# Token MLP of the first row's pairs within that row: more steps per iteration, the third pair too, and another copy on ScalarE

## The chip, the cores and the metric

The kernel runs on one core of one Trainium2 chip. The metric is the device time of one execution in microseconds. Three runs of the kernel before took 1360.49, 1360.82 and 1363.06 us; the median, 1360.82 us, is what the changed kernel is compared with. The profiled execution took 1359.68 us, of which 1357.6 us lie between the first and the last instruction. Times in the trace count from the first instruction.

## The reference

Attention with a threshold comes first, then a mixer MLP over tokens and over channels, all in float32. There are 8 batch rows, 8 heads, 576 tokens, head size 64, so a row is a 576 x 512 matrix for the MLPs.

```python
scores = matmul(q, k.T) / sqrt(64)
thresh = max(scores, axis=-1) - tau
scores = where(scores >= thresh, scores, -1e9)
attn = exp(scores - max(scores, axis=-1))
attn = attn / (sum(attn, axis=-1) + 1e-9)
x = matmul(attn, v)                          # heads side by side: 8 x 576 x 512
h = maximum(x.transpose(0, 2, 1) @ w_tok1, 0) @ w_tok2      # 576 -> 256 -> 576, over tokens
u = x + h.transpose(0, 2, 1)
out = u + maximum(u @ w_ch1, 0) @ w_ch2                     # 512 -> 1536 -> 512, over channels
```

The token MLP treats every channel by itself. So it can be made for a pair of heads (128 channels) as soon as the attention of that pair is done for all tokens; the channel MLP needs all four pairs of a row.

## The kernel before

*Units.* Heads are taken two at a time (a pair, 128 channels). The main loop (from L568) runs over 144 units of 128 queries, 18 per batch row: units 0 to 8 are pairs 0 and 1 of row 0, units 9 to 17 its pairs 2 and 3, and so on. Unit 4 of each nine is shared: 64 queries of one pair and 64 of the next. The order of all instructions on every engine is written by hand, by the order of the calls in the loop; each engine takes its own queue in that order.

*One iteration u.* `scores(u)` makes the score matmuls on PE (L303), the row maxima on DVE (L308) and a bias on GpSimd (L309). `weigh(u)` makes Prelu (L318) and Exp (L325) on ScalarE. `norm(u - 1)` takes reciprocals on DVE (L332, L333) and multiplies on GpSimd (L336). Then unit u - 2 is turned, so that keys lie on the partitions. In row 0 `turn` does that on PE in three parts of three transposes each (L354), each part copied from PSUM by DVE or by ScalarE (L356). From row 1 on `turn_blocks` does it by a transposition of blocks on DVE (L366) and, after every third unit, 16 DMAs issued by SyncE (L375).

*Values.* After every third unit `values` multiplies with v on PE (L409, L414). In row 0 this is at u = 5, 8, 11, 14, 17 and 20, called visits; the result is copied to the tile `xT` by DVE (L421). After u = 11 pairs 0 and 1 of row 0 are complete, after u = 17 pair 2, after u = 20 pair 3. In a visit, `weigh(u)` is called ahead of the turns.

*Token MLP.* `token_mlp` returns a list of steps, each with the cost in microseconds that the planner takes for it: transposes on PE (L445) that ScalarE copies to `x_sb` (L446); two steps `tok1` of PE matmuls (L452) with a relu on ScalarE (L453); and steps `tok2` (L459) that DVE adds to `xT` (L463), two for each pair.

*Where the steps run.* `push(b)` (L533), after a row is complete, queues steps in `todo`; `fill` runs them in later iterations, a share of `quota` at a time, so that the queue is spread over the next 18 iterations (less 20 us of it after row 0, `KEEP_FIRST`, and 45 us after later rows). Row 0 has a queue of its own, `early`: after u = 11 the steps of pairs 0 and 1 go there (L601), and in each iteration without a visit one of them is taken (L587): at u = 12, 13, 15, 16, 18 and 19. What is left goes to `todo` at u = 20, with the steps of pairs 2 and 3 and then the channel MLP of the first two chunks of 256 tokens (`ch1`: L483, L484; `ch2`: L499).

*PSUM.* Two buffers with the tag "tr" serve the turns, the values, the transposes of the token MLP and, until u = 18, also `tok1` and `tok2`. Row 0 has a third score buffer (`ps_3rd`); at u = 18 it is given up, and two buffers "mm" take the matmuls of both MLPs. From then on the score matmuls of u wait until Prelu of u - 1 has read its buffers.

*Weights.* All weights arrive as 64-bit numbers. In rows 0 and 1 they are brought to float32 by `weight`: a load (L177), two steps on ScalarE (L192, L194), three on DVE (L202, L204, L208) and one on GpSimd (L216) for each of 31 pieces. Row 0 takes 2.25 DVE steps per iteration; from u = 18 on it is six, two ahead of the turns, two after, two at the end. `prep` transposes q and k of the next pair on DVE (L285).

Of the kernel before, what the change touches and what calls it, by code (L numbers as in the profile page):

```python
# [21 lines left out]
def kernel(  # L22
# [25 lines left out]
    nc = tc.nc  # L48
# [10 lines left out]
    NP = H // 2  # L59
# [26 lines left out]
    UB = 9 * NP // 2  # L86
# [137 lines left out]
    def weight(n):  # L224

        nonlocal steps_done
        for k in range(steps_done, min(steps_done + n, 3 * len(pieces) + 1)):
            i, part = divmod(k, 3)
            if part == 0:
                on_gpsimd(i - 1)  # L230
                if i:
                    load_piece(i - 1 + NRAW)
            else:
                on_scalar(i + 1, part - 1)
            on_vector(i, part)
            steps_done = k + 1

    def weight_to(x):

        weight(max(int(x) - steps_done, 0))  # L240
# [36 lines left out]
    def in_blocks(b):  # L277
        return b > 0
# [50 lines left out]
    def norm(u):  # L329
        e, rs = st[u]  # L330
        rr = small.tile([P, 2], F32, tag="rr", name=f"rr_{u}")
        nc.vector.tensor_scalar(out=rr, in0=rs, scalar1=1e-9, scalar2=None, op0=ALU.add)  # L332
        nc.vector.reciprocal(out=rr, in_=rr)  # L333
        for h in range(2):
            eh = e[:, S * h : S * h + S]
            nc.gpsimd.tensor_scalar(out=eh, in0=eh, scalar1=rr[:, h : h + 1], scalar2=1.0, op0=ALU.mult, op1=ALU.mult)  # L336
        st[u] = e

    GU = 3

    def turn(u, third):

        b, p0, t = units[u]
        key, place = (b, p0, t // GU), t % GU
        e = st[u]

        if third == 0 and place == 0:
            eTs[key] = work.tile([P, NK, GU * P], F32, tag="T", name=f"eT_{u}")
        if third == 2:
            st.pop(u)  # L350
        ps = ps_tr.tile([P, MAIN], F32, tag="tr", name=f"tr{third}_{u}")[:, 0 : 3 * P].rearrange("p (c x) -> p c x", c=3)
        for c in range(3):
            k0 = (3 * third + c) * P
            nc.tensor.transpose(out=ps[:, c, :], in_=e[:, k0 : k0 + P], identity=ident)  # L354
        on = nc.scalar.copy if third == 1 else nc.vector.tensor_copy
        on(out=eTs[key][:, 3 * third : 3 * third + 3, P * place : P * place + P], in_=ps)  # L356

    def turn_blocks(u):
# [18 lines left out]
    def split_middle(n):  # L377

        lv, vl = vals[n], vlast[n % VL]
        for h in range(2):  # L380
            r = slice(D * h, D * h + D)
            nc.gpsimd.tensor_copy(out=vl[r, r], in_=lv[r, NI, :])
        vals[n] = lv, vl
# [144 lines left out]
            credit = 0.0  # L528


    early = deque()

    def push(b):  # L533
        nonlocal quota
        uT = xTs[b]
        steps, waits = token_mlp(b) if b else token_mlp(b, range(NP // 2, NP))
        old = list(todo)
        todo.clear()
        todo.extend(early)
        early.clear()  # L540

        for i, step in enumerate(steps):
            n = 2 if i in waits else 1
            todo.extend(old[:n] + [step])
            del old[:n]
        todo.extend(old)
        for i in range(2) if b % 2 == 0 else range(2, (2 * S + GR - 1) // GR):
            todo.extend(channel_mlp(b - b % 2, uT, i))
        quota = (sum(c for c, _ in todo) - (KEEP if b else KEEP_FIRST)) / (UB - 1)
# [6 lines left out]
    def values_due(u):  # L556
        while due and due[0][0] <= u:
            _, b, p0, g = due.popleft()
            values(b, p0, g)
            if b == 0 and p0 == 0 and g == 2:  # L560
                return True
            if p0 == NP - 2 and g == 2:
                if not in_blocks(b):
                    return True
                push(b)
        return False

    for u in range(len(units) + LAG + 4):  # L568
        on = u < len(units)
        if u == UB:  # L570
            late.close()
            ps_mm = ctx.enter_context(tc.tile_pool(name="ps_mm", bufs=2, space=bass.MemoryType.PSUM))
        if on:
            b_now, p0, t = units[u]
            n = b_now * NP + p0
        w = u - LAG
        back = 0 <= w < len(units)
        if on:
            scores(u)

        last = False
        visit = False
        if due and not in_blocks(due[0][1]):
            visit = due[0][0] <= u
            last = values_due(u)
        elif early:
            early.popleft()[1]()  # L587
        if 0 < u <= len(units):
            norm(u - 1)
        if b_now:  # L590
            weight(2)
        else:


            weight_to(2.25 * (u - (1 if visit else 1.5)))
            if visit and on:
                weigh(u)
        while copies:
            copies.popleft()()
        if last and u < UB:  # L600
            early.extend(token_mlp(0, range(NP // 2))[0])  # L601
        elif last:
            push(0)
        if back:
            wb, wp, wt = units[w]
            if not in_blocks(wb):
                for i in range(3):
                    turn(w, i)
            if wt % GU == GU - 1:
                g = wt // GU  # L610
                if g < 2:
                    split_middle(wb * NP + wp + g)
                due.append((u + (2 if in_blocks(wb) else 1), wb, wp, g))
        if b_now:
            fill(0.4)
        if back and in_blocks(wb):
            turn_blocks(w)
        if b_now:
            weight(2)
        if on and (b_now or not visit):  # L620
            weigh(u)
        elif b_now:
            fill(0.6)
        if b_now:
            weight(2)
        elif u == 0:
            on_scalar(0, 0)
            on_scalar(0, 1)
        else:
            weight_to(2.25 * (u - 1))  # L630
        if on:


            when = {3: (2, 0, 2), 4: (2, 2, 4), 5: (2, 4, 6), 6: (2, 6, 8), 8: (3, 0, 3), 0: (1, 3, 6), 1: (1, 6, 8)}
            if u == 0:
                load_qk(1, (nc.sync, nc.sync), range(0, 3))
            if t in when:
                m, lo, hi = when[t]
                if n + m < len(pairs):
                    load_qk(n + m, (nc.scalar if b_now else nc.sync,) * 2, range(lo, hi))  # L640
            if t in (3, 7) and n + 2 + t // 4 < len(pairs):
                load_v(n + 2 + t // 4)
            if t == 2:
                prep(n + 1)
            if t == 7 and n + 2 < len(pairs):
                prep(n + 2)
        if due and in_blocks(due[0][1]):
            values_due(u)
# [31 lines left out]
```

## Time and profile before

| part of the profile | value |
|---|---|
| span, median time | 1357.6 us, 1360.82 us |
| PE, DVE, ACT, POOL busy | 97%, 42%, 43%, 26% |
| score matmuls of u = 0, 12, 18, 20 start at | 7.14, 64.42, 98.50, 112.08 us |
| of u = 21, 24, 27, 36 | 125.36, 148.59, 173.37, 238.66 us |
| PE idle from 57.65 to 112.08 us | 54.43 - 45.37 = 9.1 us |
| PE idle from 112.08 to 183.68 us | 71.60 - 66.02 = 5.6 us |
| L452, 10 matmuls of 256 columns, at u = 16 | 2.4 us |
| L459, 12 matmuls (three steps), at u = 20 | 3.2 us |

A line of the timeline gives start and duration in microseconds, engine, line of the code, operation, output and inputs, shapes and a count; in brackets stands how long the engine was idle before it and what ended that. PEld are the weight loads of PE, which overlap its matmuls. In the trace one float32 matmul of the code is two matmuls, so a `tok1` step is 10 and a `tok2` step 4. A window's line gives, for each engine, busy time and count of instructions, then the granted clock of PE, the share of the DMA engines and GB/s. In the chain of waits each piece is the work or wait that the next one was released by.

### The profile page before, as it was taken

The numbers are of one execution on the slowest core, as the hardware profiler recorded it, in microseconds if no ns is written. First come the engines' busy times: TensorE is split into PE (matmuls) and PEld (weight loads), VectorE is DVE, ScalarE is ACT, GpSimd is POOL, SyncE is SP. The second block draws the span as 40 slices with busy tenths as digits, with TensorE's granted clock in tenths as the row PEclk, the third lists the DMA queues.
The fourth block names the chain that finished last, engine by engine and source line by source line (L and its number), as shares of the span: only waits on it lengthen the run. The fifth ranks groups of instructions, "written<-read, shape, count | busy, mean of one in ns | idle before, by whom it ended". The sixth has DMA issues, their size and how long they took to land.

```text
span 1357.6 us, 17717 instructions
## 1 busy us (share of the span) xinstructions
PE 1314.2 (97%) x6246; PEld 816.6 (60%) x6246; DVE 576.6 (42%) x1008; ACT 585.5 (43%) x1300; POOL 354.1 (26%) x683
## 2 busy tenths in 40 slices
PE   6888999999999999999999999999999999999998
PEld 4555656547474656655665566565756576576675
DVE  6889864454444434443333454434333443201000
ACT  6776655445454444543434445343434444120010
POOL 4565643222322222221212222221212222100000
PEclk8998999999999999999999999999999999999999
DMA  5435774545453533533254445435333442400000
GB/s 122 117 95 134 198 166 98 128 95 118 104 127 79 131 90 89 131 80 86 66 119 93 103 98 117 96 75 117 89 92 73 116 98 70 111 0 16 8 16 16
DMA packets 278872, 128.21 MB, mean 94 GB/s; under 512 B 200896, under 2 KB 271552, under 8 KB 278784
## 3 DMA queue, kind: packets, MB, share of 16 engines
q1 hardware_dynamic: 150176, 111.06, 32.1%
q10 hardware_dynamic: 128608, 16.01, 7.4%
q8 instruction: 50, 0.82, 0.3%
q14 instruction: 38, 0.31, 0.1%
HBM read 43.25 MB, written 9.44 MB: 39 GB/s over the span
## 4 chain that ended last, share of the span: by engine, by line
PE 86%; DVE 6%; DMA 2%; ACT 2%; SPq 2%; issue 1%; POOL 1%; ACTq 0%; DVEq 0%; POOLq 0%
PE c L499 27%; PE c L483 26%; PE sc L303 10%; PE pv L414 8%; PE t L452 5%; PE t L459 4%; PE pv L409 3%; SPq L375 2%; DVE mx L308 2%; PE tx L445 1%; PE c L495 1%; DMA lk<-in_k_dram 1%; ACT e L318 1%; ACT e L325 1%; PE tr L354 1%
## 5 line engine op out<-in xcount | busy, mean ns | idle before, releaser
L308 DVE TENSOR_REDUCE mx<-sc 128x1 f32<-128x576 f32 x288 | 204.3, 750 | 482.8 <-PE sc L303 482.8
L483 PE MATMUL c<-xT,wc 128*128 128x256 f32 (+1 forms) x1920 | 400.1, 362 | 0.5 <-ACT g L484 0.4
L499 PE MATMUL c<-wc,g 128*128 128x512 f32 x864 | 390.6, 597 | 0.0
L483 PEld LDWEIGHTS c<-xT,wc 128*128 128x128 f32 x1920 | 334.1, 190 | 71.0 <-issue 30.8
L309 POOL TENSOR_SCALAR bias<-mx,toff 128x1 f32<-128x1 f32 x288 | 82.0, 285 | 779.4 <-DVE mx L308 724.7
L318 ACT ACTIVATE e<-sc,bias 128x576 f32<-128x576 f32 x288 | 199.5, 740 | 157.5 <-POOL bias L309 154.8
L499 PEld LDWEIGHTS c<-wc,g 128*128 128x128 f32 x864 | 157.4, 190 | 175.4 <-issue 173.7
L484 ACT ACTIVATE g<-c 128x256 f32<-128x256 f32 (+1 forms) x240 | 87.1, 363 | 321.6 <-PE c L483 295.2
L325 ACT ACTIVATE e<-e,ntau 128x576 f32<-128x576 f32 x288 | 221.0, 771 | 0.0
L336 POOL TENSOR_SCALAR e<-e,rr 128x576 f32<-128x576 f32 x288 | 215.1, 760 | 14.7 <-DVE rr L333 3.0
L303 PE MATMUL sc<-kT,qT 64*128 64x288 f32 (+1 forms) x1280 | 190.5, 432 | 12.4 <-DVE kT L285 7.1
L366 DVE STREAM_TRANSPOSE T<-e 128x1152 f32<-128x1152 f32 x126 | 172.0, 1365 | 6.1 <-DMA eT<-T 3.7
L303 PEld LDWEIGHTS sc<-kT,qT 64*128 64x128 f32 (+1 forms) x1280 | 105.3, 177 | 98.7 <-issue 60.6
L414 PE MATMUL pv<-eT,lv 128*64 128x384 f32 (+1 forms) x1024 | 137.2, 408 | 0.0
L414 PEld LDWEIGHTS pv<-eT,lv 128*64 128x64 f32 x1024 | 75.6, 138 | 50.4 <-issue 40.9
L504 DVE COPY o<-c 128x512 f32<-128x512 f32 x36 | 24.7, 687 | 170.0 <-PE c L499 170.0
L419 ACT COPY xT<-pv 128x384 f32<-128x384 f32 (+1 forms) x56 | 21.0, 400 | 166.4 <-PE pv L414 165.3
L459 PE MATMUL t<-w,a 128*128 128x288 f32 x256 | 75.7, 423 | 5.7 <-DVE xT L463 4.8
L452 PE MATMUL t<-x_sb,w 128*128 128x512 f32 (+1 forms) x180 | 72.4, 549 | 0.0
L463 DVE TENSOR_TENSOR xT<-xT,t 128x288 f32<-128x288 f32 x64 | 28.4, 447 | 86.7 <-PE t L459 86.2
L459 PEld LDWEIGHTS t<-w,a 128*128 128x128 f32 x256 | 46.4, 194 | 28.4 <-issue 11.7
L325 ACT ACTIVATION_READ_ACCUMULATOR e<-e,ntau 128x1 f32 x288 | 56.7, 197 | 0.0
(43 smaller groups left out, 548.5 us busy)
## 6 DMA issues: line engine op xcount, KB each, us to landing
eT<-T SPq DMA_DIRECT2D x672, 108.0 KB, 2.3
scratch<-in_moe_w_ch_dram SPq DMA_DIRECT2D x24, 512.0 KB, 3.8
lv<-in_v_dram SPq DMA_DIRECT2D x32, 288.0 KB, 3.3
out_dram<-o SPq DMA_DIRECT2D x36, 256.0 KB, 2.2
lk<-in_k_dram ACTq DMA_DIRECT2D x111, 72.0 KB, 2.7
lq<-in_q_dram ACTq DMA_DIRECT2D x106, 72.0 KB, 2.3
lq<-in_q_dram SPq DMA_DIRECT2D x22, 72.0 KB, 3.4
lk<-in_k_dram SPq DMA_DIRECT2D x17, 72.0 KB, 3.4
```

The lines of the kernel that those rows point to most:

```text
L303: nc.tensor.matmul(sc[h][rows, f, 0:HS], lhsT=qT[r, cols], rhs=kT[r, HS * f : HS * f + HS], start=True, stop=True)
L308: nc.vector.tensor_reduce(out=mx[:, c], in_=sc[h][:, :, 0:HS], axis=AX.XY, op=ALU.max)
L318: nc.scalar.activation(out=eh, in_=sc[h][:, :, 0:HS], func=AF.Prelu, bias=bias[:, h : h + 1], scale=SCALE, alpha=STEEP)
L325: nc.scalar.activation(out=eh, in_=eh, func=AF.Exp, bias=ntau, accum_out=rs[:, h : h + 1])
L336: nc.gpsimd.tensor_scalar(out=eh, in0=eh, scalar1=rr[:, h : h + 1], scalar2=1.0, op0=ALU.mult, op1=ALU.mult)
L366: nc.vector.transpose(out=T[:, :, place, :].rearrange("p a (c x) -> p c a x", c=NK), in_=e.rearrange("p (c a x) -> p c a x", c=NK, a=4))
L414: nc.tensor.matmul(to[r], lhsT=lv[:, j, :], rhs=e[j], start=False, stop=(c == NI - 1), skip_group_check=True)
L452: nc.tensor.matmul(to, lhsT=w1[:, t, P * m : P * m + P], rhs=x_sb[:, t, cols], start=(t == 0), stop=(t == NT - 1))
L459: nc.tensor.matmul(to, lhsT=a[:, m, P * c : P * c + P], rhs=w2[:, m, HS * f : HS * f + HS], start=(m == 0), stop=(m == NTK - 1))
L483: nc.tensor.matmul(ps, lhsT=wc1[:, j, c, :], rhs=uT[:, c, GR * i : GR * i + n], start=(c == 0), stop=(c == NCC - 1))
L484: nc.scalar.activation(out=s["g"][:, j, 0:n], in_=ps, func=AF.Relu)
L499: nc.tensor.matmul(flat, lhsT=s["g"][:, j, P * t : P * t + P], rhs=wc2[:, j, :], start=False, stop=(j == NJ - 1), skip_group_check=True)
```

## The change

Three edits, all in row 0.

- *Several steps per iteration.* Where an iteration without a visit took one step from `early`, it takes steps until their planned costs reach 1.9.
- *The third pair.* After the values at u = 17, pair 2 is complete, and its token MLP is put into `early` by itself; it runs at u = 18 and 19. At u = 20 `push(0)` then queues only pair 3. Both are made with 128 columns in `x_sb` and in the `tok1` matmuls, in place of 256 for the two together.
- *The copy on ScalarE.* Of the three parts of a turn, ScalarE copied the second and DVE the other two. Now ScalarE copies the first in iterations without a visit, and the second still in visits.

The purpose is to use row 0, where PE is not yet full, for work that else waits until row 1, and to have the copies ready when PE needs a buffer.

```diff
-    def turn(u, third):
+    def turn(u, third, scalar):
...
-        on = nc.scalar.copy if third == 1 else nc.vector.tensor_copy
+        on = nc.scalar.copy if third == scalar else nc.vector.tensor_copy
...
     def push(b):
...
-        steps, waits = token_mlp(b) if b else token_mlp(b, range(NP // 2, NP))
+        steps, waits = token_mlp(b) if b else token_mlp(b, [NP - 1])
...
     def values_due(u):
...
-            if b == 0 and p0 == 0 and g == 2:
+            if (b, p0, g) in ((0, 0, 2), (0, NP - 2, 1)):
                 return True
...
-        elif early:
-            early.popleft()[1]()
+        else:
+            spent = 0.0
+            while early and spent < 1.9:
+                cost, step = early.popleft()
+                spent += cost
+                step()
...
         if last and u < UB:
-            early.extend(token_mlp(0, range(NP // 2))[0])
+            early.extend(token_mlp(0, [NP - 2] if early or u > UB - 4 else range(NP // 2))[0])
...
-                    turn(w, i)
+                    turn(w, i, 1 if visit else 0)
```

In the order of the changed kernel, with NP = 4 and UB = 18, iteration 12 takes three transposes and the first `tok1` of pairs 0 and 1, 13 the second `tok1`, 15 and 16 two `tok2` each; 18 takes the transposes and both `tok1` of pair 2, 19 its two `tok2`; 20 takes all of pair 3. The matmuls of the channel MLP begin at u = 21 in place of 22.

## The prediction

> **What bounds the kernel now.** I read first the page's busy shares and its slices, then the busy time by stage, then the order of time around the change, and last the chain of waits. "u" is the iteration of the main loop, one block of 128 queries; row 0 is u = 0 to 17, and its copying goes on to u = 20. On PE, iteration u starts with the score matmuls of L303; in the timeline they start at 64.42 us (u = 12), 98.50 (18), 112.08 (20), 125.36 (21), 142.04 (23), 173.37 (27), 238.66 (36).
>
> The page: PE is full after the first few slices, and only there are DVE, ACT and POOL busy too.
>
> ```profile
> PE 1314.2 (97%) x6246; PEld 816.6 (60%) x6246; DVE 576.6 (42%) x1008; ACT 585.5 (43%) x1300; POOL 354.1 (26%) x683
> PE   6888999999999999999999999999999999999998
> DVE  6889864454444434443333454434333443201000
> PEclk8998999999999999999999999999999999999999
> ```
>
> So after some 180 us the time is PE's work, and what counts is what is left to do then and when that moment comes. Busy time by stage (u = 11 to 19, 20 to 27, 28 to 35):
>
> ```profile
> core 0: us, PE busy (x) PEld busy (x) DVE busy (x) ACT busy (x) POOL busy (x), PEclk, DMA share, GB/s
> 57.65:112.08 54.43, 45.37 (x277) 28.91 (x276) 44.77 (x93) 42.98 (x88) 34.57 (x52) 0.97 0.50 123
> 112.08:183.68 71.60, 66.02 (x324) 43.48 (x323) 62.11 (x101) 45.80 (x97) 45.02 (x53) 0.95 0.65 173
> 183.68:238.66 54.98, 53.75 (x242) 32.31 (x240) 29.22 (x48) 29.38 (x66) 18.02 (x37) 1.00 0.51 117
> ```
>
> In the first stage no engine is full (PE 83%, DVE 82%, ACT 79%): they wait for each other. In the second PE (92%) and DVE (87%) are both near full. In the third PE is the bound. How the first stage waits is seen in the timeline of u = 12:
>
> ```profile
> 65.59 0.66 PE L445 MATMUL tx<-ident,xT 128*128 128x128 f32 x4
> 66.29 0.59 ACT L446 COPY x_sb<-tx 128x512 f32<-128x512 f32 x1 [1.53 <-PE tx L445]
> 67.51 0.48 ACT L356 COPY eT<-tr 128x384 f32<-128x384 f32 x1
> 68.04 0.55 PE L354 MATMUL tr<-ident,e 128*128 128x128 f32 x3 [0.57 <-ACT eT L356]
> 68.52 1.35 PE L303 MATMUL sc<-kT,qT 64*64 64x288 f32 x16
> ```
>
> Turns, values and token steps share two PSUM buffers ("tr"), so each step put ahead of the turns is followed by a copy that the turns wait for, and the next scores stand behind the turns in PE's queue. The chain of waits from u = 21 on runs for 36 us through DVE, SP and a weight load, hardly through PE:
>
> ```profile
> 129.27 1.36 DVE T L366
> ...
> 137.94 1.29 DVE T L366
> 139.23 1.04 DVE wc L208
> 140.27 0.39 DVE h L202
> 140.66 0.18 SPq L375
> ...
> 150.86 3.90 DMA scratch<-in_moe_w_ch_dram
> ...
> 171.44 1.99 PE c L483 x8
> ```
>
> **What the Trainium skill says.** "TensorE: Matmul & The Clock Gate", section "Architectural detail": ACT and DVE take their queues strictly in order. The trace agrees: scores' maxima (L308) stand behind whatever weight step came before. The same page, "LDWEIGHTS": a load costs by its columns, 128 / 1.2 = 107 ns. The trace has three loads for the turns in 0.31 us, 103 ns each, so 128-column matmuls can be fed. "SBUF — State Buffer", "Who interferes with whom": some DVE copies and scalar steps lock a port that GpSimd needs. The same L204 takes 0.43 us at 128.91 and 1.40 us at 105.77, while POOL's L216 runs.
>
> **The change part by part.**
>
> *ScalarE copies part 0 of a turn outside visits.* Part 2 of a turn waits for ScalarE's copy before and after. Part 0 is ready some 0.4 us ahead of part 1, so where ScalarE is idle the turn ends up to 0.6 us sooner. At u = 2 it is idle (1.71 us before its copy at 19.16) and DVE's queue (transposes, maxima) follows directly: -0.6. At u = 3 to 10 ScalarE is late with its weight steps (u = 4, 7, 10), or DVE sets the next maxima: 0. The number of copies on each engine is unchanged.
>
> *Steps of pairs 0 and 1 bunched.* Before: one step each at u = 12, 13, 15, 16, 18, 19, three left for u = 20. After (order of the changed kernel): three transposes and one L452 group at u = 12, the other group at 13, two token-2 steps (L459) at 15 and two at 16. I lay these on the trace's queues with its durations: L452, 10 matmuls of 256 columns, 2.4 us; a token-2 step, 4 matmuls, 1.06; x_sb copies 0.55 and 0.37; relu 0.38; L463 0.45.
> - u = 12: PE transposes to 66.6, ScalarE copies to 67.7, L452 to 69.8, relu to 70.3, ScalarE's weight step (0.67) and its turn copy to 71.4, last turn part at 71.44, next scores 71.9 instead of 68.52: +3.4.
> - u = 13: a second L452 group takes the place of four transposes and their late copy: +0.3, total 3.7. u = 14: the wait for POOL's vl copy (0.5) and the one before it are over by then: -1.0.
> - u = 15: two token-2 steps, whose L463 stand behind the maxima on DVE and give the turns their buffers: 4.85 us instead of 3.64: +1.2. u = 16: two of them against an L452 group: 0. u = 17: DVE waited 0.66 without cause there: -0.3. Total at u = 18 +3.6 (-0.6 of u = 2 apart).
>
> *Pair 2 within the row, u = 18 and 19.* At 18: five transposes, two copies (0.58, 0.3), two L452 groups of 128 columns, two relus, all ahead of the turns; before one L452 group. The 128-column cost is in the trace: L483 in that shape runs 8 matmuls in about 1.0 us, so a group of 10 takes 1.2, half of 2.4: no loss from halves. Chain: scores end +1.2, copies +2.7, groups +5.0, relu +5.3, weight step +5.9, turn copy +6.4, last part on DVE +7.6 from the start; before +5.7 (103.66 to 104.2): +1.8, total 5.4. Behind that copy DVE has L208, L202, L204, L208 (3.7 us as before) and then the maxima of u = 19, so DVE hands on all of it. u = 19: one L463 more, one wait for PE (0.64) less: 0.
>
> *Pair 3 at u = 20.* Now all six steps stand between the values (L409, L414) and the next scores. Each waits for the last: xT copy (DVE, behind the maxima, rr, L202, L204), transposes, x_sb copy, two groups, relu, token-2. Of this PE waits some 2.5 us for the xT copy, 0.7, 0.9 and 0.3 for ScalarE. DVE stands at the two L463, which come ahead of its last weight steps, the transposes of q and k and the maxima of u = 21: it is done with L202 some 4 us before the first, where before it waited 1.4 us in all at u = 20. I take +3.2 for the maxima of u = 21 (bounds: 0, if the pair's chain ends while DVE still has work; 5, if PE runs the values at the slow rate of before, 5.0 us instead of 3.6). Total 8.6.
>
> *Row 1, u = 21 to 26.* Five token-2 steps less there; DVE loses three L463 up to the maxima of 23 (1.35) and a wait (0.2): -1.7. PE has less to do but DVE and the chain shown (L366 of u = 22, 16 issues of eT on SP, the weight load, its steps) set the pace: nothing more. Total 6.9 at u = 23, and it stays to u = 27. L463, L446 and L453 moved to row 0 are in the sums above.
>
> *Row 1, u = 27 to 35.* Work queued at the push falls from 96.7 to 89.1 planner units (three token-2 steps of 0.97 and half of 9.4 gone; a unit is about 1.05 us in the trace: 0.97 stands for a step of 1.06, 1.72 for an L483 group of 1.79), so each iteration fills 4.06 instead of 4.51. Nine iterations at PE's bound: 9 x 0.45 = -4.0. From u = 36 the remaining work is the same (20 units kept) and PE is full: the shift is final.
>
> Sum: -0.6 + 3.4 + 0.3 - 1.0 + 1.2 - 0.3 + 1.8 + 3.2 - 1.7 - 4.0 = +2.3; 1360.8 + 2.3 = 1363.1 us.
>
> **The rivals.**
> - *Row 0 takes the work into its idle time.* PE is idle 8.9 of 47.7 us at u = 12 to 19, and 8.3 us of PE work move in (three token-2 steps 3.2, pair 2's two groups 2.4, its two token-2 steps 2.1, transposes 0.6). If three quarters of the idle time (6.7 us) takes it up, the row grows by 8.3 - 6.7 = 1.6 in place of 5.4; with half of u = 20's wait, -0.6 + 1.6 + 1.6 - 1.7 - 4.0 = -3.1: 1357.7; with no growth and no wait, -6.3: 1354.5. For it: idle time of that size. Against: PE's idle time is waits for ScalarE and DVE in the same loop that the added steps lengthen.
> - *Only u = 20's wait is hidden* (DVE finds work, the queues recover by 27): 2.3 - 3.2 = -0.9: 1359.9.
> - *More is lost.* If the stalls at u = 19 and 20 keep the slow clock (PEclk was 0.77 and 0.87 there), +1.4, and two more L204 fall on L216 (1.40 for 0.43), +2: 2.3 + 3.4 = 5.7: 1366.5.
>
> **How the numbers follow.** Forecast 0.45, with its sum just under the 2.7 us that 0.2% is: 0.20 of it slower, 0.25 the same. Row 0 takes it in: 0.25, faster. u = 20 hidden: 0.10, same. More lost: 0.20, slower. Faster 0.25, same 0.35, slower 0.40. The range goes from 1355.5 (all but the best of the first rival) to 1368 (past the last by the 1.5 us that the bound of u = 20 leaves).
>
> **What would show it.** Scores of u = 13, 18, 20, 21 at about 71.3, 101.5, 116, 131 (before 68.52, 98.50, 112.08, 125.36); a DVE wait of 3 us or more for L463 at u = 20; scores of u = 27 near 180 and of u = 36 near 241; L452's 128-column groups at 1.2 us. I am wrong if u = 18 starts within 1 us of before, if no such wait is there, or if u = 27 to 36 doesn't get shorter by about 4.

## The result and the profile after

The changed kernel takes 1379.12 us (1377.43 to 1380.39) beside 1361.53 us of the kernel before on the same chip: 1.0129 times as long, 95% interval 1.0114 to 1.0144. The forecast of 1363.1 us and the upper end of the range, 1368.0, were both too low. The medians are 17.6 us apart; the two profiled executions, from which the tables below are made, are 19.6 us apart (spans of 1357.6 and 1377.2 us). Three executions of the experiments below ran far longer than their like and are in no figure: one of e3 at a granted clock of 0.755 (1707.35 us, the one that was profiled) and two of e15 (2689.7 and 3515.47 us).

The page of the changed kernel, busy totals and slices:

```profile
PE 1320.3 (96%) x6266; PEld 821.4 (60%) x6266; DVE 575.0 (42%) x1008; ACT 585.5 (43%) x1303; POOL 353.5 (26%) x683
PE   6888688999999999999999999999999999999998
DVE  5877764444444443434243444434333443201000
PEclk9999899999999999999999999999999999999999
```

In the fifth slice (138 to 172 us) PE falls from 9 to 6 and the clock to 8, and in the next two slices PE is at 8 where it was at 9; DVE's busy stretch is lower. From the eighth slice on PE looks as before. The windows of the changed kernel (u = 11 to 19, 20 to 27, u = 24 by itself, 28 to 35) say how large it is:

```profile
core 0: us, PE busy (x) PEld busy (x) DVE busy (x) ACT busy (x) POOL busy (x), PEclk, DMA share, GB/s
58.52:118.40 59.88, 51.63 (x321) 34.04 (x320) 45.18 (x98) 45.30 (x95) 35.24 (x52) 0.99 0.46 113
118.40:199.14 80.74, 64.06 (x304) 40.76 (x304) 61.17 (x96) 43.45 (x93) 44.37 (x53) 0.92 0.56 154
154.15:174.41 20.26, 15.29 (x53) 9.10 (x53) 9.64 (x15) 9.58 (x21) 5.94 (x7) 0.75 0.69 197
199.14:255.53 56.39, 52.49 (x234) 31.76 (x234) 28.48 (x48) 28.03 (x64) 18.05 (x37) 0.97 0.49 114
```

The middle stage has fewer matmuls than before (304 for 324) and takes 9.1 us more (80.74 for 71.60). The growth of u = 24 alone is larger than that: it takes 20.26 us where it took 9.70. The last stage has 8 matmuls less (234 for 242) and takes 1.4 us more: PE, idle for 1.23 us there before, is now idle for 3.90.

Laid out by the starts of the scores, in the stretches that the prediction used, the 19.6 us between the two profiled spans are:

| iterations | predicted | measured | how it is read |
|---|---|---|---|
| start of u = 0 | 0 | +1.6 | 8.7 for 7.1, before any changed instruction |
| u = 0 to 19 | +4.8 | +4.7 | u = 20 at 118.40 for 112.08, less the 1.6 |
| u = 20 | +3.2 | 0.0 | 13.29 for 13.28 |
| u = 21 and 22 | -1.7 | -2.8 | 13.84 for 16.68 |
| u = 23 to 26 | 0 | +10.0 | 41.32 for 31.33; of it u = 24 is 20.26 for 9.70 |
| u = 27 to 35 | -4.0 | +3.4 | 68.68 for 65.29 |
| u = 36 to the end | 0 | +2.7 | the rest |

Two executions of the same instructions can differ by some us, so this table needs a second look. Up to u = 20, five of the profiled kernels have the code of the kernel before (itself, e6, e11, e16 and e17): from the start of u = 0 to that of u = 20 they take 104.9 to 108.3 us, in the mean 106.7. Six have the code of the changed kernel (itself, e5, e8, e9, e10 and e14): 109.7 to 113.8 us, in the mean 111.6. The growth of row 0, not quite 5 us, is thus no matter of the two executions in the table; a difference of 1 or 2 us between single iterations can be (u = 24 takes 9.3 us in e11 and 11.4 in e17, and up to u = 27 both have the code of the kernel before).

Row 0 went as worked out. Its timeline at u = 12 of the changed kernel:

```profile
66.46 1.09 PE L445 MATMUL tx<-ident,xT 128*128 128x128 f32 x8
67.16 1.45 ACT L446 COPY x_sb<-tx 128x512 f32<-128x512 f32 x3 [1.53 <-PE tx L445]
68.28 2.43 PE L452 MATMUL t<-x_sb,w 128*128 128x256 f32 x10
71.59 0.46 ACT L356 COPY eT<-tr 128x384 f32<-128x384 f32 x1
72.10 0.55 PE L354 MATMUL tr<-ident,e 128*128 128x128 f32 x3 [0.38 <-ACT eT L356]
72.58 1.35 PE L303 MATMUL sc<-kT,qT 64*64 64x288 f32 x16
```

Transposes, copies and the `tok1` group all stand ahead of the last turn part, and the scores of u = 13 come 7.30 us after those of u = 12 instead of 4.10. Then the chain of waits of the changed kernel at the place that was not foreseen:

```profile
158.93 1.47 POOL e L336 x2
160.40 4.72 DMA scratch<-in_moe_w_ch_dram
165.15 0.04 issue
165.20 0.67 ACT scratch L192
165.87 0.27 ACT g L484
166.14 0.14 issue
166.27 3.75 PE c L483 x8
170.03 1.48 PE pv L409 x4
171.50 2.97 PE pv L414 x16
174.48 1.22 PE sc L303 x8
```

In the kernel before, the weight load led into the chain too; here a relu (L484) and a whole `ch1` group (L483) have been put between that load and the next scores. The timeline of u = 24 shows who stands behind whom:

```profile
148.34 11.26 SPq L375 DMA_DIRECT2D eT<-T  x16
156.71 4.59 PE L483 MATMUL c<-xT,wc 128*128 128x256 f32 x16
159.71 10.01 SPq L177 DMA_DIRECT2D scratch<-in_moe_w_ch_dram  x5
163.89 0.67 ACT L192 ACTIVATE scratch<-scratch 128x512 int32<-128x512 uint32 x1 [7.39 <-DMA scratch<-in_moe_w_ch_dram]
165.77 0.36 ACT L484 ACTIVATE g<-c 128x256 f32<-128x256 f32 x1
166.27 3.75 PE L483 MATMUL c<-xT,wc 128*128 128x256 f32 x8 [4.97 <-ACT g L484]
174.41 1.24 PE L303 MATMUL sc<-kT,qT 64*128 64x288 f32 x8
```

Two `ch1` groups run and fill both "mm" buffers. The third needs the relu of the first; that relu stands on ScalarE behind weight steps (L192), which wait for their loads, and SyncE could issue these only after the 16 issues of eT (the last of them ends at 159.6 us, the first load is issued at 159.71). The same place in the kernel before:

```profile
149.76 3.72 PE L483 MATMUL c<-xT,wc 128*128 128x256 f32 x16
153.41 0.87 PE L409 MATMUL pv<-eT,vl 128*64 128x384 f32 x4
154.79 0.70 ACT L192 ACTIVATE scratch<-scratch 128x512 int32<-128x512 uint32 x1 [5.21 <-DMA scratch<-in_moe_w_ch_dram]
158.29 1.86 PE L303 MATMUL sc<-kT,qT 64*128 64x288 f32 x8 [1.44 <-ACT e L318]
```

There u = 24 has two groups. It ran into the same late step (L192 waited 5.21 us), but PE had nothing in its queue that needed the relu, and went on to the values; only the next scores waited, 1.44 us, for Prelu (L318), which stands behind the same step. In the changed kernel PE stands still for 4.97 us. Then it runs slowly: the eight matmuls of the third group take 3.75 us, where the groups ahead of the stall take 1.8 to 2.3 each. The Trainium skill ("TensorE: Matmul & The Clock Gate", section "Part 1: The HAM clock gate", under "What's actually happening") says that PE drops to half its clock after an idle window of about 3.4 us; the granted clock of 0.75 in this window and the doubled time of the group agree.

### The profile page after: what moved, and what is told of

Its sections match the earlier page's. It is cut to its first block, busy times and chain, and to the rows that moved or that the text cites. A ratio compares the mean times of both kernels' runs of the same rounds, so it can differ in the third digit from the quotient of the medians.

```text
span 1377.2 us, 17765 instructions
## 1 busy us (share of the span) xinstructions
PE 1320.3 (96%) x6266; PEld 821.4 (60%) x6266; DVE 575.0 (42%) x1008; ACT 585.5 (43%) x1303; POOL 353.5 (26%) x683
## 4 chain that ended last, share of the span: by engine, by line
PE 84%; DVE 6%; SPq 3%; DMA 3%; ACT 3%; issue 1%; POOL 1%; ACTq 0%; DVEq 0%; POOLq 0%
PE c L483 25%; PE c L499 24%; PE sc L303 11%; PE pv L414 8%; PE t L452 5%; PE t L459 4%; PE pv L409 3%; SPq L375 3%; DVE mx L308 2%; PE tx L445 1%; PE c L495 1%; ACT e L318 1%; PE tr L354 1%; DMA eT<-T 1%; DMA scratch<-in_moe_w_ch_dram 1%
## 5 line engine op out<-in xcount | busy, mean ns | idle before, releaser
L483 PE MATMUL c<-xT,wc 128*128 128x256 f32 (+1 forms) x1920 | 402.0, 363 | 5.0 <-ACT g L484 5.0
L483 PEld LDWEIGHTS c<-xT,wc 128*128 128x128 f32 x1920 | 335.6, 191 | 76.3 <-issue 33.3
L318 ACT ACTIVATE e<-sc,bias 128x576 f32<-128x576 f32 x288 | 199.4, 739 | 162.3 <-POOL bias L309 158.7
L484 ACT ACTIVATE g<-c 128x256 f32<-128x256 f32 (+1 forms) x240 | 86.7, 362 | 329.8 <-PE c L483 319.2
L303 PE MATMUL sc<-kT,qT 64*128 64x288 f32 (+1 forms) x1280 | 193.8, 436 | 17.5 <-ACT e L318 8.8
L366 DVE STREAM_TRANSPOSE T<-e 128x1152 f32<-128x1152 f32 x126 | 172.1, 1366 | 6.3 <-DMA eT<-T 2.8
L303 PEld LDWEIGHTS sc<-kT,qT 64*128 64x128 f32 (+1 forms) x1280 | 106.7, 179 | 105.6 <-issue 59.1
L459 PE MATMUL t<-w,a 128*128 128x288 f32 x256 | 74.2, 417 | 2.9 <-DVE xT L463 1.0
L452 PE MATMUL t<-x_sb,w 128*128 128x512 f32 (+2 forms) x200 | 72.8, 513 | 1.2 <-ACT x_sb L446 1.1
L463 DVE TENSOR_TENSOR xT<-xT,t 128x288 f32<-128x288 f32 x64 | 28.3, 446 | 81.4 <-PE t L459 80.7
L459 PEld LDWEIGHTS t<-w,a 128*128 128x128 f32 x256 | 45.3, 190 | 26.0 <-issue 11.9
L409 PE MATMUL pv<-eT,vl 128*64 128x384 f32 (+1 forms) x256 | 46.3, 431 | 13.3 <-DMA eT<-T 6.9
```

What stands on the lines that cost most here:

```text
L303: nc.tensor.matmul(sc[h][rows, f, 0:HS], lhsT=qT[r, cols], rhs=kT[r, HS * f : HS * f + HS], start=True, stop=True)
L318: nc.scalar.activation(out=eh, in_=sc[h][:, :, 0:HS], func=AF.Prelu, bias=bias[:, h : h + 1], scale=SCALE, alpha=STEEP)
L366: nc.vector.transpose(out=T[:, :, place, :].rearrange("p a (c x) -> p c a x", c=NK), in_=e.rearrange("p (c a x) -> p c a x", c=NK, a=4))
L409: nc.tensor.matmul(to[r], lhsT=vl[:, r], rhs=e[NI], start=True, stop=False, skip_group_check=True)
L452: nc.tensor.matmul(to, lhsT=w1[:, t, P * m : P * m + P], rhs=x_sb[:, t, cols], start=(t == 0), stop=(t == NT - 1))
L459: nc.tensor.matmul(to, lhsT=a[:, m, P * c : P * c + P], rhs=w2[:, m, HS * f : HS * f + HS], start=(m == 0), stop=(m == NTK - 1))
```

## The experiments

Three theories stand behind the expectations. **R**: the third `ch1` group at u = 24 waits for a relu that stands behind a weight step whose load is late. **L**: the late load alone holds u = 24, whatever the groups. **Q**: row 1 is not at PE's bound when it is given less to fill (a smaller quota), so the work that left it shortened nothing. A ratio is always to the runs of the kernel before on the same chip.

### Which edit it is

The copy alone, on the kernel before (e1_copy_only):

```diff
-    def turn(u, third):
+    def turn(u, third, scalar):
-        on = nc.scalar.copy if third == 1 else nc.vector.tensor_copy
+        on = nc.scalar.copy if third == scalar else nc.vector.tensor_copy
```

> The kernel before with the third edit alone: ScalarE copies the first part of a turn outside visits. Prediction's step: -0.6 us, so 1361 us. Both theories of the loss at u = 24 (relu behind the load; late load) say the same, since nothing of the channel MLP or of the weights moves: 1360 to 1362 us.

1361.94 us, ratio 0.9991 (0.9981 to 1.0). That is -1.2 us, with an interval from -2.6 to 0, which holds the -0.6 of the prediction: at most a small gain.

The third pair alone, with one step per iteration (e7_third_only):

```diff
-        steps, waits = token_mlp(b) if b else token_mlp(b, range(NP // 2, NP))
+        steps, waits = token_mlp(b) if b else token_mlp(b, [NP - 1])
...
-            if b == 0 and p0 == 0 and g == 2:
+            if (b, p0, g) in ((0, 0, 2), (0, NP - 2, 1)):
...
-            early.extend(token_mlp(0, range(NP // 2))[0])
+            early.extend(token_mlp(0, [NP - 2] if early or u > UB - 4 else range(NP // 2))[0])
```

> The kernel before with the second edit alone: pair 2's token MLP queued by itself at u = 17, pair 3's by itself at u = 20, but one step per iteration, so that only one transposition and one matmul step more than none run early and pair 2's steps mostly reach row 1. Two L483 groups at u = 24. If halves of 128 columns cost nothing (prediction's step) and u = 24 is what counts: 1360 to 1364 us. If the halves or their waits cost: 1366 us or more.

1363.25 us, ratio 1.0003 (0.9994 to 1.0013). So halves of 128 columns and the other order of pairs 2 and 3 cost nothing.

Both of these together, that is the changed kernel with one step per iteration again (e12_no_bunch):

```diff
-        else:
-            spent = 0.0
-            while early and spent < 1.9:
-                cost, step = early.popleft()
-                spent += cost
-                step()
+        elif early:
+            early.popleft()[1]()
```

> The changed kernel with one step per iteration again (edits 2 and 3 alone; two L483 groups fall on u = 24). If the several steps per iteration are the cause of all that was lost: 1360 to 1364 us, as the third pair alone (1363.25) and the copy alone (1361.94) would make it, with u = 24 at some 10 us. If halves, pair 3 or the interplay of the edits cost by themselves: 1366 or more.

1363.29 us, ratio 0.9997 (0.9984 to 1.0009): level with before. Without the several steps per iteration the whole loss is gone. And they by themselves, on the kernel before (e2_bunch_only, the same diff the other way round):

> The kernel before with the first edit alone: several token steps of pairs 0 and 1 per iteration, pairs 2 and 3 still made together at u = 20. Its u = 24 takes three L483 groups where the kernel before takes two. Theory R (the third group needs a PSUM buffer whose relu stands on ScalarE behind a weight step that waits for its load; values and scores of u = 25 stand behind the group on PE): u = 24 takes 16 us or more in place of 9.7, and the kernel 1367 to 1373 us. Theory L (the weight load itself comes late because DVE and the SP queue reach it late, whatever PE does): the load comes only some 2 to 4 us later than before, 1362 to 1365 us.

1385.67 us, ratio 1.016 (1.014 to 1.018): more than the whole loss, and more than was expected. u = 18 starts 4.7 us later against u = 0, u = 24 takes 18.1 us and PE's third group there waits 4.21 us for its relu. With this kernel it is settled which edit costs, but not how. What the orders show is that the steps taken early are missing in the queue that is pushed at u = 20: the quota is smaller and the channel MLP begins earlier. In e12 its groups fall on u = 22 to 26 as in the kernel before (1, 3, 2, 3, 3), while e2 and the changed kernel have three at u = 24.

### The stall at u = 24

The changed kernel with at most two groups at u = 24 (e3_two_at_24, and once more as e10_cap_again):

```diff
+    LIMIT = {24: 2}
+    taken = {}
...
         while todo and credit > 0:
+            if taken.get(u, 0) >= LIMIT.get(u, 99):
+                break
+            taken[u] = taken.get(u, 0) + 1
             cost, step = todo.popleft()
```

> The changed kernel with at most two planned steps at u = 24; the third L483 group goes to u = 25. All work is still done. R: PE passes the values and reaches the scores of u = 25 some 7 us sooner, u = 24 takes about 13 us in place of 20.3, and the kernel about 1372 us. L: the load comes as late as before, DVE and ScalarE start u = 25 no sooner, 1378 to 1380 us.

> The same kernel as the one with two L483 groups at u = 24 (the changed kernel otherwise), for an undisturbed trace beside the next two. If the third group's wait at u = 24 is what was lost, the time is again about 8 us under the changed kernel: 1370 to 1374 us, u = 24 takes 13 to 15 us instead of 20.3, and the scores of u = 36 start 8 to 11 us after those of before. If the earlier 8 us were chance, 1376 to 1380.

1374.83 us, ratio 1.0071 (1.0045 to 1.0096), and 1375.17 us, ratio 1.0094 (1.0073 to 1.0115). Only the trace of the second is used. Both lie under the changed kernel, by 4 to 8 us (the intervals of the second and of the changed kernel just touch); u = 24 takes 13.9 us instead of 20.3. So R is part of it, and half of the loss or more is elsewhere.

The other way round: the kernel before, with one group more drawn to u = 24 (e6_before_three):

```diff
+        if u == 24 and share == 0.4:
+            credit += 1.72
```

> The kernel before with one L483 group moved from u = 25 to u = 24, so that u = 24 takes three. No other edit. Theory R (the third group waits for a relu behind the late weight step, and values and scores stand behind it): u = 24 takes 14 us or more in place of 9.7, the kernel 1365 to 1370 us. Theory L (the late load alone counts): u = 24 as before, and the kernel 1362 to 1364 us.

1366.8 us, ratio 1.0032 (1.0018 to 1.0046). The stall appears in a kernel that had none. In its timeline, the weight step and the third group:

```profile
156.46 0.67 ACT L192 ACTIVATE scratch<-scratch 128x512 int32<-128x512 uint32 x1 [6.25 <-DMA scratch<-in_moe_w_ch_dram]
158.94 3.46 PE L483 MATMUL c<-xT,wc 128*128 128x256 f32 x8 [4.96 <-ACT g L484]
```

u = 24 grows from 9.7 to 16.6 us, but at the end only 4.4 us are left (2.5 to 6.3): the group drawn forward is missing in a later iteration.

The cap with several steps per iteration alone (e13_bunch_cap: the diffs of e2 and e3 together):

> The kernel before with several steps per iteration alone, and at most two L483 groups at u = 24 (that edit without the limit took 1385.67). If the third group at u = 24 is the larger part of what this edit costs: 1368 to 1376, with u = 24 at 13 us or less in place of 18.1. If the loss is the order in row 0 and the later idle time of PE, and the third group little: 1380 to 1386.

1378.09 us, ratio 1.011 (1.0096 to 1.0124): 7.6 us less than without the cap, but more than the 1368 to 1376 expected, and u = 24 still takes 15.1 us, over the 13 expected. With its two groups PE is idle there for 6.18 us: 2.94 at the values, for eT, and 3.24 at the next scores, for a Prelu that stands behind L192. So a late load costs something by way of Prelu too, without a third group; that much of L stays.

To test the order, the changed kernel keeps its three groups and its late load, and only the weight steps move behind relu and Prelu (e14_steps_later). They move on DVE as well as on ScalarE:

```diff
-            weight(2)
+            weight(0 if u == 24 else 2)
...
-            weight(2)
+            weight(0 if u == 24 else 2)
...
-            weight(2)
+            weight({23: 0, 24: 8}.get(u, 2))
```

> The changed kernel with the eight weight steps of the end of u = 23 and the first two places of u = 24 made at the end of u = 24 instead: three L483 groups stay at u = 24, the load comes as late, but relu and Prelu no longer stand behind the ScalarE step that waits for it. If the order on ScalarE is what stalls PE: u = 24 takes 10 to 13 us in place of 20.3, PE's wait for the relu is under 1 us, and the total falls by 4 to 9 us, to 1370 to 1375. If the late load holds the iteration in another way (by DVE or by the weights), u = 24 stays above 16 us and the total above 1376.

1377.49 us, ratio 1.0108 (1.0092 to 1.0123). In u = 24 of its timeline PE waits for nothing:

```profile
157.19 6.77 PE L483 MATMUL c<-xT,wc 128*128 128x256 f32 x24
164.33 0.68 ACT L192 ACTIVATE scratch<-scratch 128x512 int32<-128x512 uint32 x1
```

All three groups run without a break, u = 24 takes 12.2 us with PE idle for none of it, and u = 27 starts 6.0 us earlier than in the changed kernel, both counted from u = 0. That settles R as the cause of PE's stall: the same groups, another order, and the first load is issued 5.0 us after the start of u = 24, where it was 5.6. L falls as the cause of this stall, since the load is about as late as before. The 8 us by which u = 24 is shorter are not all the relu's, for on DVE, too, a wait of 6.37 us behind the same weight steps no longer stands ahead of the block transposition. And the total did not do what R expected (1370 to 1375): of the 6 us only 2 to 3 are left at the end, and the interval overlaps that of the changed kernel. The windows of the same kernel for u = 24 and for u = 28 to 35:

```profile
155.10:167.30 12.20, 12.20 (x54) 7.75 (x54) 7.11 (x13) 8.45 (x19) 4.87 (x7) 0.86 0.87 263
192.90:251.60 58.70, 53.92 (x234) 32.20 (x234) 28.65 (x48) 28.14 (x64) 18.06 (x37) 0.94 0.47 109
```

u = 28 to 35 now takes 58.70 us, 2.3 more than in the changed kernel. PE arrives early at the first matmuls of the values (L409) in that stretch and waits there (the last figures are the idle time ahead of them, in us, and what ended it):

```profile
L409 PE MATMUL pv<-eT,vl 128*64 128x384 f32 x8 | 2.4, 685 | 4.8 <-DMA eT<-T 4.8
```

The same move on the kernel before, together with the copy (e15_before_later):

> The kernel before with the copy on ScalarE (1361.94 by itself) and the same eight weight steps moved to the end of u = 24. PE was idle 1.43 us in u = 24 of before. Expected 1359.5 to 1362 us: at most 1.5 us gained by the move; if the moved steps then hold the maxima of u = 25 or the weights, a loss of 1 to 4: 1363 to 1366.

1363.76 us, ratio 1.0002 (0.999 to 1.0014): no gain, although PE's 1.43 us of idle time at u = 24 are gone.

Two attempts at L take the wait away from the load. The weight loads of row 1 issued by GpSimd, so that eT does not stand ahead of them (e4_load_pool), and half of eT's issues on GpSimd (e8_eT_split):

```diff
-        nc.sync.dma_start(out=like(raw, dst), in_=src)
+        (nc.gpsimd if b_now else nc.sync).dma_start(out=like(raw, dst), in_=src)
```

```diff
-                    nc.sync.dma_start(out=eT[32 * a : 32 * a + 32, :, i, :], in_=T[32 * i : 32 * i + 32, a, :, :])
+                    (nc.gpsimd if i % 2 else nc.sync).dma_start(out=eT[32 * a : 32 * a + 32, :, i, :], in_=T[32 * i : 32 * i + 32, a, :, :])
```

> The changed kernel with the weight loads of rows 1 on issued by GpSimd, right behind the step that frees their buffer, in place of SyncE, where they stand behind the 16 issues for eT. Takes away what makes the load late. R and L both: the wait of ScalarE's weight step at u = 24 (7.4 us) mostly goes, so does the stall of PE, and the kernel takes 1366 to 1371 us. If the loss at u = 24 has another cause, or GpSimd's issue costs as much as it saves: 1378 us or more.

> The changed kernel with the 16 issues of eT after every third unit split between SyncE and GpSimd, 8 each. SyncE is then free about 5 us sooner for the weight load of u = 24 and for the next. Theory L: the wait of ScalarE there falls from 7.4 to some 2 us and with it PE's stall and the waits of the values for eT: 1366 to 1371 us. If GpSimd's issues (0.6 to 0.9 us each beside its busy queue in row 1) delay the products that the transpositions wait for: 1378 us or more.

1385.13 us, ratio 1.0156 (1.0122 to 1.019), and 1378.87 us, ratio 1.0121 (1.0102 to 1.014). In both the stall is gone (u = 24 takes 13.1 and 12.9 us), and the total is no better. In the first PE waits elsewhere, three times by 3 us at the values (u = 27, 30 and 33) and by 2.78 us at the scores of u = 24; in the second PE is idle for 10.8 us in u = 20 to 23, where the changed kernel had 7.5. Like e14, they say that time won at u = 24 is not kept.

The second is also a test of eT in the rest of row 1. Its 16 issues take 5.7 to 7.2 us, and PE waits for eT at no values from u = 24 to 35. Yet u = 28 to 35 takes 56.18 us, where the changed kernel takes 56.39. Its timeline at u = 31 to 33:

```profile
225.24 4.36 POOL L375 DMA_DIRECT2D eT<-T  x8 [0.77 <-issue]
229.97 1.37 ACT L318 ACTIVATE e<-sc,bias 128x576 f32<-128x576 f32 x2 [2.20 <-POOL bias L309]
230.77 1.86 PE L303 MATMUL sc<-kT,qT 64*128 64x288 f32 x8 [1.69 <-ACT e L318]
```

GpSimd's own issues hold up the bias, so Prelu and the next scores wait in eT's place. So this kernel does not say what would be won if eT came early and nothing else came late.

### What row 1 is bound by

The prediction took nine iterations of row 1 to be 4.0 us shorter, because each has 0.45 planner units less to fill. First, the changed kernel with two groups at u = 24 and the old quota of 4.51 (e5_keep_two: the cap, and `KEEP_FIRST = 12.35`):

> The changed kernel with at most two planned steps at u = 24, as in the run before with two (1374.8 us, 1.0071), and with KEEP_FIRST 12.35 in place of 20, so that the quota is 4.51 again and row 1 gets the same planned work per iteration as before. Theory Q (with the smaller quota PE outruns the DMAs of eT and the queue of DVE in row 1 and idles there, so work taken out of row 1 is not gained): the work put back fills idle time, and what is left for later falls by 7.65 us: 1366 to 1370 us. Rival (row 1 is bound by PE, as the prediction had it): the order of work is moved and no work is saved, 1371 to 1375 us.

1380.62 us, ratio 1.0136 (1.0111 to 1.0162), worse than with the cap alone. Its timeline has other waits at u = 26 and 27:

```profile
184.85 1.12 PE L499 MATMUL c<-wc,g 128*128 128x512 f32 x2 [2.56 <-POOL wc L216]
192.77 2.01 PE L499 MATMUL c<-wc,g 128*128 128x512 f32 x2 [2.92 <-POOL wc L216]
196.92 2.07 PE L499 MATMUL c<-wc,g 128*128 128x512 f32 x2 [2.13 <-POOL wc L216]
```

With the channel MLP an iteration early and a full quota, `ch2` reaches weights that GpSimd has not yet converted: 7.6 us in three waits. That hid what was asked. So the quota was changed only after the weights are done, at u = 28, up in the changed kernel with the cap (e9_cap_late) and in the kernel before (e11_before_late), and down in the kernel before to the 4.06 of the changed one (e17_before_less, with -0.45):

```diff
         if b_now:
+            if u == 28:
+                quota += 0.95
             fill(0.4)
```

> Two L483 groups at u = 24, and from u = 28 on 0.95 planner units more per iteration, so that u = 28 to 35 fill 5.0 in place of 4.06. The total of PE work is unchanged. Theory Q (with the smaller quota PE has too little to fill the waits of row 1, so it idles; the reckoned -4.0 was lost so): PE's idle time from u = 28 to 36 falls from some 5 to under 2 us, and the total falls by 3 to 6 us against the same kernel without it: 1365 to 1370. Rival (PE is the bound in u = 28 to 35 whatever is filled, as the prediction had it): u = 36 starts some 8 us later, the rest is that much shorter, and the total is unchanged within 1.5 us: 1370 to 1374.

> The kernel before with the same 0.95 planner units more per iteration from u = 28 on. PE is idle there for only 1.2 of 55 us (183.68 to 238.66). Both theories: u = 36 starts later by about 8 us and the total stays within 1.5 us of before, 1360 to 1363. A fall of 3 us or more would say that a larger quota is worth something by itself, and not because the change had left PE idle.

> The kernel before with 4.06 instead of 4.51 planner units per iteration in u = 28 to 35 (3.6 units less; they are made in row 2). PE's bound, as the prediction had it: u = 28 to 36 gets 3.8 us shorter (55.0 to some 51), PE idle there stays near 1.2 us, the total is unchanged: 1361 to 1363.5. Theory Q (the rest of the iteration, values waiting for the DMAs of eT above all, does not get faster, so PE idles): u = 28 to 36 is shortened by less than 2 us, PE idle there rises to 3 to 5 us, and the total grows by 2 to 4 us: 1364 to 1367.

1372.8 us, ratio 1.0077 (1.0056 to 1.0099); 1364.65 us, ratio 1.0013 (1.0003 to 1.0024); and 1370.36 us, ratio 1.0058 (1.0042 to 1.0074). The third answers most of the question. Nothing but the quota differs, from u = 28 on, and the kernel is 8 us slower, more than the 2 to 4 that Q expected. Its window for u = 28 to 35:

```profile
189.30:245.40 56.10, 51.04 (x228) 29.39 (x226) 28.52 (x48) 27.63 (x63) 18.12 (x37) 0.97 0.49 114
```

14 matmuls fewer than before (228 for 242), PE busy for 2.7 us less, and yet 1.1 us longer: PE is idle for 5.06 us instead of 1.23. Other kernels agree: with the quota of the kernel before, u = 28 to 35 takes 53.7 to 55.0 us (before, e1, e7, e12, e15), and with that of the changed kernel 56.1 to 58.7 (itself, e4, e8, e10, e14). The exception is e16 below, at 53.4. The groups of L409, the first matmuls of the values, in the same iterations, tell where; first the kernel before, then e17, the changed kernel, and e9 (the last figure is the idle time ahead of them):

```profile
L409 PE MATMUL pv<-eT,vl 128*64 128x384 f32 x8 | 1.7, 508 | 1.2 <-DMA eT<-T 1.2
```

```profile
L409 PE MATMUL pv<-eT,vl 128*64 128x384 f32 x8 | 2.2, 635 | 5.1 <-DMA out_dram<-o 3.7 <-DMA eT<-T 1.4
```

```profile
L409 PE MATMUL pv<-eT,vl 128*64 128x384 f32 x8 | 1.7, 504 | 3.9 <-DMA lq<-in_q_dram 2.4 <-issue 1.5
```

```profile
L409 PE MATMUL pv<-eT,vl 128*64 128x384 f32 x8 | 1.7, 512 | 0.0
```

The values need eT, and eT has a time of its own: the last block transposition (L366), 16 issues by SyncE in 10.3 to 13.0 us, and the landing. From that transposition to the values, where PE waits for them, it is 15.4 us in the kernel before, 14.4 and 14.1 in the changed one, 13.4 and 17.0 in e17. The lines put the wait down once to eT, once to other transfers that ended near it. The traces decide it: where PE waits at L409 in these kernels, the last of the 16 transfers of eT landed 0.04 to 0.4 us before L409 began; in e9, where it doesn't wait, 0.9 us and more before. With less filling that interval does not get shorter by as much as the work, and PE arrives early; with more filling (e9) the wait is gone, and PE's idle time in u = 28 to 35 falls from 3.60 us in e10 to 0.00.

In e9 the total falls by only 2.4 us against e10, less than Q had expected, and with overlapping intervals; in e11 the larger quota costs 2 us. PE is idle for longer in the rows behind: from u = 54 to 142 by 4.65 us in e9 for 1.71 in e10, and 5.62 in e11 for 1.22 in before. So these two attempts to fill row 1 by borrowing from the rows behind it gained nothing that is clear of the noise.

Last, the kernel before with the smaller quota from the push at u = 20 on (e16_before_keep, `KEEP_FIRST = 27.65`):

> The kernel before with KEEP_FIRST 27.65, so that the quota is 4.06 from the push at u = 20 on; two L483 groups stay at u = 24. PE's bound: 1361 to 1363.5. Theory Q: PE idle in u = 25 to 36 rises from 1.6 to 4 us or more and the total by 3 to 8 us: 1365 to 1371.

1373.93 us, ratio 1.0087 (1.0069 to 1.0105). u = 20 to 35 takes 126.50 us with 533 matmuls, where the kernel before takes 126.60 with 565. The 32 matmuls taken out of row 1 bought nothing there, and were paid for later: u = 36 to 53 takes 5.1 us more than before and u = 54 to 142 6.9 more, with 16 of these matmuls in each. The loss, expected at 3 to 8 us, is 12, as large as that of the changed kernel without its stall (e10, 1.0094).

## Why the prediction was wrong

**Row 0, right.** The copy was put at -0.6: u = 3 starts 0.6 to 0.7 us sooner after u = 0 in the changed kernel and in each kernel with that edit. u = 12 was put at +3.4 and is +3.2 (7.30 for 4.10), u = 15 at 4.85 us and is 4.84; u = 18 was put at +1.8 and is +1.3. The two 128-column groups were put at 2 x 1.2 us and take 2.50 for both, 125 ns a matmul. The Trainium skill ("TensorE: Matmul & The Clock Gate", section "LDWEIGHTS") puts a weight load of 128 columns at 107 ns; the 20 loads of these groups take 2.31 us, 116 ns each, so they keep up with the matmuls. The sum up to u = 19 is +4.8 predicted and +4.7 measured. So PE's idle time of row 0 did not take up the work, as the first rival would have had it: of 9.1 us of idle time there, 8.25 are still there after.

**u = 20, too dear.** It was predicted at +3.2 and is 0.0 (13.29 for 13.28). The xT copy was expected to hold PE for 2.5 us and held it for 0.60; DVE waited 2.0 us for the two L463 instead of 3. So the second rival was right on this step. u = 21 and 22 gave -2.8 instead of -1.7 (there are four token-2 steps less in them, not five). These two errors, 4.3 us together, lie on the other side (u = 23 starts 1.9 us later, where 6.3 was summed): without them the forecast would have missed by more.

**u = 23 to 26, the step that failed.** "PE has less to do but DVE and the chain shown ... set the pace: nothing more. Total 6.9 at u = 23, and it stays to u = 27." It was put at 0 and is +10.0. The chain was named, with its load and L192. L192 came 9.1 us later (163.89 for 154.79), 3.5 more than the start of u = 24. What was not asked is what else lies behind L192 on ScalarE. With the channel MLP one iteration earlier and the smaller quota, its groups fall differently on the iterations: 3, 2, 2, 3 at u = 21 to 24 instead of 1, 3, 2 at u = 22 to 24. That put a third group, with two buffers, into just the iteration whose relu waits for a load. That was in the order of the changed kernel, and could have been read there. u = 24 grew by 10.6 us, with a wait of 4.97 us for the relu and slow matmuls after it; e6 and e14 show the cause, and e3 and e10 that 4 to 8 us of it reach the end.

**u = 27 to 35, the other step that failed.** "Nine iterations at PE's bound: 9 x 0.45 = -4.0." The measured figure is +3.4. PE was 98% busy in u = 28 to 35 (53.75 of 54.98 us), and the prediction took that for a bound that moves down with the work. e17 and e16 show that it doesn't. In e17 the filling had just covered the way of eT, and with less of it PE waits there; in e16 PE's idle time in u = 20 to 35 grows from 6.8 to 11.0 us, in waits of several kinds. In the changed kernel it begins at u = 27, which takes 12.29 us for 10.31: PE waits 2.75 us at the values for eT and then 1.49 at the scores of u = 28 for Prelu. One sign was in the trace of before: in u = 28 to 35, the only idle time of PE was 1.2 us ahead of L409, waiting for eT. So PE was not alone the bound; eT took about as long. Whether eT is the only thing that does is open, since in e8 its waits go and others take their place.

**After u = 36, taken as final.** It was +2.7 us more, none of it in row 2 (137.94 us for 138.00). Kernels with another quota in row 1 have 4 to 6 us of PE's idle time from u = 54 to 142, where the kernel before has 1.22 (the changed kernel 2.05). It comes with less filling as with more. Part of it recurs at fixed places: at u = 63, 99 and 135 PE can wait 0.82 us before L459 for the relu of the `ch1` group ahead of it, once in the kernel before and in the changed one, at all three in e9, e11 and e17; most of the rest are waits at the values. What decides where they fall is not settled. For that reason the 8 us of e17 and the 12 of e16 are explained only in part: against the kernel before, e17 takes 1.1 us more in u = 28 to 35, 1.5 in u = 36 to 53 and 5.1 in u = 54 to 142.

Of the three signs of being wrong that the prediction named, the first stayed away (u = 18 starts 2.9 us later after u = 0). The other two came: DVE's wait at u = 20 was 2.0 us and not 3, and u = 27 to 35 did not get shorter. The rivals reached 1366.5 us at most. All of them looked for the loss where steps were added. It was made in u = 24 and in the iterations after it, by waits that none of them asked for.

A version better than both kernels did not come out of this: the copy on ScalarE by itself, at 0.9991, is the nearest.

## What to carry to other kernels

A stage with PE at 98% is PE-bound only as far as nothing else takes as long: look at the one wait that is left in it (here 1.2 us ahead of L409), for here that wait grew when PE got less to do. When work is taken out of a filler queue, look at where each later step lands: by the iteration, with the number of buffers, and with what waits in order ahead of the copy or relu that frees them. And work taken out of a stage where it covered a way of transfers was no gain there in this kernel, while it was paid for where it went.

## What was not expected

- The stall of PE of 5 us cost more than itself: after it, eight matmuls took 3.75 us (3.46 in e6) for 1.8, and the values 4.45 us (169.96 to 174.41) for the 3.45 that they took in the kernel before.
- To issue by GpSimd what SyncE issued (e4, e8) removed the wait it was meant for and gained nothing; in e8 the eight issues took GpSimd 4.36 us, and the bias stood behind them.
- The very first scores start at 7.1 to 7.4 us in some executions and at 8.4 to 9.1 in others, with the same code up to there: 1.6 of the 19.6 us between the two profiled spans are of that kind.
